# Which tiles the split planes of the last two FFN groups are put in

## The chip, the cores and the metric

The kernel runs on one core of a Trainium2 chip. The metric is device time in microseconds (us), as the median of the runs; lower is better. The engines are TensorE (PE in the profile; its weight loads are PEld), VectorE (DVE), ScalarE (ACT), GpSimd (POOL) and SyncE (SP, which issues DMAs).

## The reference

Eight batches of eight heads of attention over 576 tokens with 64 dimensions, in which scores below the row's maximum less `tau` are dropped, and then a feed-forward network (FFN) with an ELU over the 4608 tokens:

```python
scores = scale * np.matmul(q, k.transpose(0, 1, 3, 2))
thresh = np.max(scores, axis=-1, keepdims=True) - tau
scores = np.where(scores >= thresh, scores, -1000000000.0)
attn = softmax(scores)                       # written out in the reference
x = np.matmul(attn, v)                       # (8, 8, 576, 64) -> (4608, 512)
h = x @ w_in                                 # (512, 2048)
g = np.where(h > 0.0, h, np.exp(np.minimum(h, 0.0)) - 1.0)
return (g @ w_out).astype(np.float32)        # (2048, 512)
```

Everything is float32.

## The kernel before

**Groups.** The FFN is done in nine groups of 512 tokens. Groups 0 to 6 are worked beside the attention. Most of them use a Strassen scheme over sums of the weights' blocks. The change touches what comes last, groups 7 and 8 (`g7`, `g8` in the code), which run after the attention's last scores.

**Split planes.** Those two groups don't multiply in float32, which the rest of the FFN does. Each operand is split into planes of type float32r (`F32R`): `cut` (L2007, ACT) makes a scaled copy, `rest` (L2011, DVE) what that copy leaves out, `cross` (L2017, DVE) a mixture of both. For weights the same is done by `weights_cut` (L2028, ACT), `weights_rest` (L2032, DVE) and `weights_cross` (L2036, DVE). A product then is three matmuls of 128 x 128 by 128 x 512: cut by cut, rest by rest and cross by cross.

**The two rounds.** First every step (group, f) of the 16 blocks f of the hidden dimension: eight matmuls for cut and rest (`first_round`, L2203) and four for cross (`cross_round`, L2216) give h in one bank of PSUM; ACT scales the bank between them (L2207). ACT (exponential, L2227), POOL (L2230) and DVE (L2233) turn it into the raw activation, a float32 tile, which is split again. The two groups' steps are interleaved, so that planes of `w_in` made for group 7 serve group 8 a little later: 32 steps, 384 matmuls. Then the second round (`second`, L2278) multiplies the activations' planes with those of `w_out`, group 7 first, then group 8: 16 blocks times four token tiles times three matmuls for each group, 384 more. The first and last three blocks of a group (`EDGE = 3`) are taken together for each token tile. The stationary operand is a plane of `w_in` in the first round and of the activations in the second; the moving operand is a plane of x, and then of `w_out`.

**Order.** A planner writes the order out by hand. `at(t, f)` puts a piece of work on an agenda at a modelled time, `on_pe(cost, f)` does all that is due and then issues matmuls, `issued(key, x)` does more of the agenda until the plane that it is asked for is there. Nothing in it looks at which tile a plane got, so the order of instructions doesn't hang on tiles.

**Room.** A plane is 128 x 512, 2 KB a partition, and takes its room by `take`, which calls `slot(dt)`. There are two kinds of room:
- *Free slots*: 24 named `r0` to `r23`, opened where the attention's tiles were (L2069), and 34 named `l0` to `l33`, opened where the Strassen tiles were (L2139). They are kept in the queue `free`. A slot taken anew is a new tile over the old one's room.
- *Dead quarters*: once a weights' tile (`w_in0` to `w_in3`, `w_out0` to `w_out3`, four times 128 x 512 each) or a token tile `xt` isn't needed any more, `give` declares its room a new tile and puts its four quarters into `kept_for[dt]`. `kept_for[FP32]` serves raw activations, `kept_for[F32R]` the planes. The latter gets `w_out0` to `w_out3` as their blocks are split (`out_done`), and `w_in3` at the end of the first round's splitting (`in_done`). In the profile a float32r plane under the name `w_out` or `w_in` lies in such a quarter.

When its last matmul has been issued, `drop` puts a plane's room at the end of the queue that it came from, and the next taker gets the room at the front. The first instruction that writes a plane into such room waits until the matmul that read the earlier plane has ended.

Of the kernel before, what the change touches and what calls it, by code (L numbers as in the profile page):

```python
# [10 lines left out]
FP32 = mybir.dt.float32  # L11
# [357 lines left out]
def kernel(  # L369
# [1245 lines left out]
    with tc.manual_schedule():  # L1615
# [353 lines left out]

        EDGE = 3
        EPS, CUT = 2.0**-12, 1.0 - 2.0**-13
        free, kept_for, parts, split_stack = deque(), {FP32: deque(), F32R: deque()}, {}, ExitStack()

# [6 lines left out]
            kept_for[dt].extend(t[:, x] for x in range(KJ))  # L1982

        def slot(dt, wide=True):
            if kept_for[dt]:
                t = kept_for[dt].popleft()
                return t, lambda: kept_for[dt].append(t)
            pool, name = home = free.popleft()
            return pool.tile([P, DM], dt, name=name), lambda: free.append(home)

        def drop(key, *which):
            for x in which or range(len(parts[key])):
                parts[key][x][1]()
# [6 lines left out]
        def take(key, dt):  # L2000
            t = slot(dt)
            parts.setdefault(key, []).append(t)
            return t[0]
# [15 lines left out]
        def split_tokens(t, key, src, then=None):  # L2019
            at(t, lambda: cut(key, src))  # L2020
            at(t + 0.8, lambda: (rest(key, src), then and then()))
            at(t + 1.5, lambda: cross(key))
# [228 lines left out]
        def g_of(g, f):  # L2251
            def src():
                while (g, f) not in raw_g:
                    do_next()
                return raw_g[g, f]

            return src

        def start_f(t0, f):
            return t0 if f < EDGE else min(t0 + UNIT * f, t0 + UNIT * (NFT - EDGE))  # L2260

        OUT_EARLY = 11
        for f in range(NFT):
            split_weights(begin + 22.0 + 3.9 * f if f < OUT_EARLY else start_f(middle, f) - 9.0, ("out", f), w_out_of(f),
                          lambda f=f: out_done(f))
            for g, t0 in ((g7, middle), (g8, end)):
                t = start_f(t0, f) - (11.5 if f < EDGE else 6.0) + 3.2 * f * (f < EDGE)
                split_tokens(t, ("h", g, f), g_of(g, f), lambda g=g, f=f: drop(("g", g, f)))
# [41 lines left out]
        for g in (g7, g8):  # L2310
            for fs in (range(EDGE), *((f,) for f in range(EDGE, NFT - EDGE)), range(NFT - EDGE, NFT)):
                for i in range(4):
# [39 lines left out]
```

## Time and profile before

| | |
|---|---|
| median of 3 runs | 1260.25 us (1260.03 to 1261.15) |
| profiled execution | 1260.53 us, span 1258.8 us |
| TensorE busy | 1246.0 us (99%) |
| VectorE, ScalarE, GpSimd busy | 1041.6, 636.3, 729.1 us |
| granted TensorE clock | 1.00 |
| first matmul of group 7, last of group 8 | starts at 1076.7, starts at 1253.9 us |
| their 768 matmuls | 177.19 us of TensorE busy in 1077.0 to 1258.8 us |

Times in the profile count from the start of the span. The drained end of one matmul overlaps the start of the next, so a group of n matmuls in the timeline is shown longer than n starts: a single one is shown as 0.39 us, while starts are some 0.23 us apart. The chain of waits counts from end to end and doesn't have this overlap. "f<-r,l" names the tile written (f, a bank of PSUM), then the two tiles read without their numbers: moving operand, stationary operand.

### The profile page before, as it was taken

The page shows a single profiled execution, that of the slowest core. Times are in us where ns is not written, and L with a number is a line of the kernel's source. Part 1 is how long each engine was busy: PE and PEld are TensorE (multiplying, and loading weights), DVE is VectorE, ACT ScalarE, POOL GpSimd, SP SyncE. Part 2 cuts the span into 40 slices and gives each one's busy share as a digit, 9 for nine tenths or more (in the row PEclk, how much of TensorE's full clock was granted, in tenths as well). Part 3 has the DMA queues.
Part 4 walks back from the last instruction along what each step waited for, and adds up shares of the span by engine and source line. Part 5 has one row for each costly group of instructions (what it writes and reads, how often), then busy time and mean ns, then how long its engine had stood idle before and what let it go on. Part 6 is the DMA issues. An engine that isn't in the chain of part 4 may idle for free.

```text
span 1258.8 us, 21129 instructions
## 1 busy us (share of the span) xinstructions
PE 1246.0 (99%) x6598; PEld 956.6 (76%) x6598; DVE 1041.6 (83%) x2199; ACT 636.3 (51%) x1331; POOL 729.1 (58%) x1061
## 2 busy tenths in 40 slices
PE   8999999999999999999999999999999999999998
PEld 6676576477788787888788788778788887788876
DVE  6888778789898988898889889898889886876785
ACT  6989776664453526253534435352625352465321
POOL 4778655687575848676576757574867655122000
PEclk9999999999999999999999999999999999999999
DMA  7456688998989898998989888989899875000001
GB/s 138 147 175 178 175 244 219 274 255 226 235 236 260 241 249 232 235 257 220 269 206 259 226 241 219 261 242 251 231 234 257 221 232 173 20 1 1 1 34 34
DMA packets 325551, 245.74 MB, mean 195 GB/s; under 512 B 209216, under 2 KB 289984, under 8 KB 325440
## 3 DMA queue, kind: packets, MB, share of 16 engines
q1 hardware_dynamic: 323264, 243.65, 72.1%
q8 instruction: 52, 0.85, 0.3%
q10 hardware_dynamic: 2176, 0.75, 0.2%
q14 instruction: 59, 0.48, 0.1%
HBM read 154.53 MB, written 89.78 MB: 194 GB/s over the span
## 4 chain that ended last, share of the span: by engine, by line
PE 90%; DVE 3%; DMA 3%; ACT 1%; issue 1%; SPq 1%; POOL 1%; DVEq 0%; ACTq 0%; POOLq 0%
PE f L1678 22%; PE f L1818 22%; PE sc L977 8%; PE sc L1050 7%; PE f L2278 6%; PE f L2203 5%; PE f L1102 4%; PE sc L673 3%; PE f L1154 3%; PE f L2216 2%; PE pv L930 2%; PE rt L792 2%; PE sc L1042 1%; DMA there<-x 1%; PE sc L1037 1%
## 5 line engine op out<-in xcount | busy, mean ns | idle before, releaser
L984 DVE TENSOR_REDUCE mx<-sc 128x1 f32<-128x576 f32 x207 | 148.3, 750 | 28.3 <-PE sc L977 24.3
L726 POOL TENSOR_SCALAR w<-w,rs 128x576 f32<-128x576 f32 x144 | 116.3, 816 | 69.6 <-DVE rs L789 69.4
L1004 ACT ACTIVATE w<-sc,mx 128x576 f32<-128x576 f32 x113 | 81.5, 740 | 115.6 <-DVE mx L984 98.7
L868 DVE STREAM_TRANSPOSE x<-w 128x512 f32<-128x512 f32 (+1 forms) x153 | 108.9, 745 | 13.8 <-POOL w L726 11.8
L996 POOL TENSOR_SCALAR th<-mx,ntau 128x2 f32<-128x2 f32 (+1 forms) x114 | 34.0, 298 | 132.6 <-DVE mx L984 132.5
L977 PE MATMUL sc<-kT,qT 64*128 64x448 f32 (+4 forms) x736 | 103.1, 416 | 0.3 <-ACT xs L1066 0.3
L977 PEld LDWEIGHTS sc<-kT,qT 64*128 64x128 f32 x736 | 80.7, 186 | 25.2 <-issue 16.2
L1011 DVE SCALAR_TENSOR_TENSOR w<-sc,th,w 128x576 f32<-128x576 f32 x113 | 88.2, 810 | 9.4 <-ACT w L1004 9.2
L1678 PE MATMUL f<-xt,sw 128*128 128x256 f32 x384 | 93.4, 386 | 0.8 <-DVE g L1700 0.8
L1678 PE MATMUL f<-xt,w_in 128*128 128x256 f32 x384 | 92.3, 383 | 0.0
L1818 PE MATMUL f<-w_out,s 128*128 128x256 f32 x384 | 92.0, 382 | 0.1
L1818 PE MATMUL f<-w_out,g 128*128 128x256 f32 x384 | 92.0, 382 | 0.0
L1678 PE MATMUL f<-x,w_in 128*128 128x256 f32 x384 | 90.9, 379 | 0.0
L1818 PE MATMUL f<-t,s 128*128 128x256 f32 x384 | 90.8, 379 | 0.0
L726 POOL TENSOR_SCALAR e<-e,rs 128x576 f32<-128x576 f32 x91 | 67.4, 744 | 35.2 <-DVE rs L789 33.8
L1678 PEld LDWEIGHTS f<-xt,sw 128*128 128x128 f32 x384 | 69.4, 189 | 17.1 <-issue 4.5
L1678 PEld LDWEIGHTS f<-xt,w_in 128*128 128x128 f32 x384 | 71.7, 190 | 12.9 <-ACT w L1692 2.3
L1818 PEld LDWEIGHTS f<-w_out,g 128*128 128x128 f32 x384 | 72.0, 190 | 12.4 <-issue 3.1
L1818 PEld LDWEIGHTS f<-w_out,s 128*128 128x128 f32 x384 | 71.9, 190 | 12.5 <-issue 2.5
L1678 PEld LDWEIGHTS f<-x,w_in 128*128 128x128 f32 x384 | 72.8, 190 | 10.5 <-ACT s L1692 0.7
L1818 PEld LDWEIGHTS f<-t,s 128*128 128x128 f32 x384 | 72.8, 190 | 10.3 <-POOL s L1765 0.4
L1765 POOL TENSOR_TENSOR s<-g 128x256 f32<-128x256 f32 x96 | 75.0, 786 | 7.9 <-DVE g L1728 7.4
(349 smaller groups left out, 3113.7 us busy)
## 6 DMA issues: line engine op xcount, KB each, us to landing
there<-x SPq DMA_DIRECT2D x444, 144.0 KB, 3.5
wTb<-there SPq DMA_DIRECT2D x58, 576.0 KB, 6.5
wTa<-there SPq DMA_DIRECT2D x53, 576.0 KB, 5.0
sw<-win_sums SPq DMA_DIRECT2D x46, 384.0 KB, 4.9
t<-wout_sums SPq DMA_DIRECT2D x33, 512.0 KB, 6.1
qm<-in_q_dram SPq DMA_DIRECT2D x124, 72.0 KB, 4.8
wst<-in_moe_w_in_dram SPq DMA_DIRECT2D x16, 512.0 KB, 4.3
vm<-in_v_dram SPq DMA_DIRECT2D x64, 128.0 KB, 3.9
```

The costliest lines, as they stand in the source:

```text
L726: nc.gpsimd.tensor_scalar(wv, wv, st["rs"][:, h : h + 1], 1.0, ALU.mult, ALU.mult)
L868: nc.vector.transpose(x[:, :, c0 : c0 + nc_], src.rearrange("p (c g n) -> p g c n", c=nc_, n=T))
L977: on_banks(nc.tensor.matmul(o, qT[r, i * P : (i + 1) * P], kT[r, k0 : k0 + n], start=True, stop=True, skip_group_check=True), o)
L984: on_banks(nc.vector.tensor_reduce(st["mx"][:, h : h + 1], st["sc", h], axis=AX.XY if i == NC else AX.X, op=ALU.max, negate=True), st["sc" ...
L1004: on_banks(nc.scalar.activation(st["e", h], st["sc", h], AF.Exp, bias=st["mx"][:, h : h + 1]), st["sc", h])
L1011: on_banks(nc.vector.scalar_tensor_tensor(st["e", h], st["sc", h], st["th"][:, h : h + 1], st["e", h], ALU.is_ge, ALU.mult, accum_out=st[" ...
L1050: on_banks(nc.tensor.matmul(o, vm[:, h, c], parts[part][:, g0:g1, h * (NC + 1) + c], start=False, stop=(c == NC - 1), skip_group_check=Tru ...
L1678: nc.tensor.matmul(loc["banks"][place], left[:, j], right[:, j], start=(begins and j == 0), stop=(j == 1), skip_group_check=True)
L1765: engine.tensor_tensor(o, x, y, op)
L1818: nc.tensor.matmul(place(m), lhs, rhs, start=(begins and v == 0), stop=(v == RU - 1), skip_group_check=True)
L2203: nc.tensor.matmul(o, w.rearrange("p (j f) -> p j f", j=KJ)[:, j], m, start=(j == 0 and x == 0), stop=(j == KJ - 1 and x == 1), skip_group ...
L2278: nc.tensor.matmul(banks8[2 * i + x // 2], h[:, tok], w, start=(f == 0 and x != 1), stop=(f == NFT - 1 and x != 0), skip_group_check=True)
```

## The change

`slot` gave a plane a dead quarter whenever there was one, and a free slot otherwise. Now a float32r plane, which TensorE reads, takes a free slot, and a dead quarter only while no more than `RESERVE` = 2 free slots are left. Raw activations (float32) are served as before: a dead float32 quarter first, else a free slot.

```diff
-        EDGE = 3
+        EDGE, RESERVE = 3, 2
...
         def slot(dt, wide=True):
-            if kept_for[dt]:
+            if kept_for[dt] and (dt is FP32 or len(free) <= RESERVE):
                 t = kept_for[dt].popleft()
                 return t, lambda: kept_for[dt].append(t)
             pool, name = home = free.popleft()
             return pool.tile([P, DM], dt, name=name), lambda: free.append(home)
```

## The prediction

> **What bounds the kernel now.** The change acts only in the last two FFN groups, so I read the page for the engine totals, then the chain of waits for that stretch, then the timeline of TensorE by tile names, then the windows.
>
> The page, and then the chain that ended last (start, length, engine, line, count):
>
> ```profile
> span 1258.8 us, 21129 instructions
> PE 1246.0 (99%) x6598; PEld 956.6 (76%) x6598; DVE 1041.6 (83%) x2199; ACT 636.3 (51%) x1331; POOL 729.1 (58%) x1061
> ```
>
> ```profile
> 1115.99 1.81 PE f L2203 x8
> 1117.80 0.91 PE f L2216 x4
> 1118.71 1.87 PE f L2203 x8
> 1120.58 0.93 PE f L2216 x4
> ...
> 1164.77 27.42 PE f L2278 x118
> ...
> 1192.88 1.91 DVE l L2032 x3
> ...
> 1200.87 0.61 DVE r L2036
> ...
> 1201.53 52.76 PE f L2278 x226
> ```
>
> The reader should see two things. TensorE is the chain: matmuls follow one another from L2203 through L2216 to L2278, whose last piece ends at 1254.29; the 4.5 us from there to the end of the span are the last block's way out, which the change doesn't touch. And one matmul of the same shape doesn't always take the same time: eight L2203 matmuls take 1.81 us (226 ns each) at 1115.99 and 1.87 us at 1118.71, and 118 L2278 matmuls take 27.42 us (232 ns each). The page's "99% busy" hides this. So a change that makes no engine idle less may still shorten the span.
>
> Which tiles the longer ones read is in the timeline of TensorE. The second name after the arrow is the stationary operand, a single name means both come from tiles of that name; l and r are free slots, w_out and w_in in these lines are dead quarters of the weights' tiles:
>
> ```profile
> 1113.10 1.98 PE L2203 MATMUL f<-r,l 128*128 128x512 f32 x8
> ...
> 1118.55 2.03 PE L2203 MATMUL f<-r,w_out 128*128 128x512 f32 x8
> 1120.42 1.09 PE L2216 MATMUL f<-r,l 128*128 128x512 f32 x4
> ...
> 1124.06 1.98 PE L2203 MATMUL f<-r,r 128*128 128x512 f32 x8
> ```
>
> Every eight with slots alone take 1.98 us here (the last one's drain included), the eight with w_out 2.03, and the four that follow them 1.09 (0.93 against 0.91 in the chain), though they read a slot. That reads like a delay begun by the quarter and worked off after it. It is told apart from mere lateness by 1124.06, which is later and quick again. Why a quarter is slower to read no row shows.
>
> The windows give the stretch as blocks of equal content (length, TensorE busy, count of records touching the window, granted clock, DMA share, GB/s):
>
> ```profile
> 1091.35:1118.55 27.20, 27.20 (x122) 1.00 0.00 1
> 1118.55:1146.07 27.52, 27.52 (x121) 1.00 0.00 1
> 1146.07:1164.61 18.54, 18.54 (x82) 1.00 0.00 0
> 1164.61:1172.97 8.36, 8.36 (x38) 1.00 0.01 2
> 1172.97:1186.91 13.94, 13.94 (x62) 1.00 0.00 0
> 1186.91:1195.27 8.36, 8.36 (x38) 1.00 0.00 0
> 1195.27:1209.50 14.23, 14.15 (x61) 1.00 0.06 20
> 1209.50:1217.89 8.39, 8.39 (x38) 1.00 0.25 94
> 1217.89:1231.81 13.92, 13.92 (x61) 1.00 0.00 1
> 1231.81:1240.19 8.38, 8.38 (x38) 1.00 0.00 0
> 1240.19:1253.87 13.68, 13.68 (x60) 1.00 0.15 38
> ```
>
> The count has records draining over the edges; matmuls that start in the windows are 120, 120, 80, then 36, 60, 36, 60, 36, 60, 36, 59 (and the last at 1253.87). The first window has no operand in a quarter: 27.20 / 120 = 226.7 ns, my base. The granted clock is 1.00 throughout, so the excess is not throttling. Nor is it DMA: it is there at a DMA share of 0.00.
>
> The only idle time of TensorE behind the first group is this:
>
> ```profile
> 1201.05 0.40 PE L2278 MATMUL f<-l,w_out 128*128 128x512 f32 x1
> 1201.39 1.28 DVE L2036 TENSOR_TENSOR l<-l,w_out 128x512 fp32r<-128x512 f32 x2
> 1201.52 0.19 PEld L2278 LDWEIGHTS f<-r,r 128*128 128x128 f32 x1 [0.51 <-DVE r L2036]
> 1201.53 0.50 PE L2278 MATMUL f<-r,r 128*128 128x512 f32 x1
> 1201.86 0.39 PE L2278 MATMUL f<-w_out,w_in 128*128 128x512 f32 x1
> ```
>
> From 1201.05 to 1201.86 lie two starts that should take 0.46: the stall costs 0.35. The chain above says where it is from: ACT's weight planes (L2028) at 1192.22, then VectorE in one piece. ACT came late because its slot was just being read:
>
> ```profile
> 1192.22 1.68 ACT L2028 ACTIVATE w_out<-w_out 128x512 fp32r<-128x512 f32 x3 [2.15 <-PE f L2278]
> ```
>
> **The change part by part.** No instruction is added, removed or moved: in the changed program every engine has the same instructions in the same order, SP's and POOL's queues and all DMA issues too, only operands lie elsewhere. The two programs' operands, counted: of the 768 matmuls 396 read a quarter before (392 as stationary, 4 as moving operand alone), and 84 after (48 and 36). By the blocks above, before and after: 0 and 0; 36 and 0; 44 and 40; then 20 and 8; 52 and 0; 36 and 16; 44 and 0; 24 and 4; 56 and 0; 36 and 16; 48 and 0.
>
> *Pace.* The excess over 226.7 ns: block two 27.52 - 27.20 = 0.32 us; block three 18.54 - 80 x 0.2267 = 0.40; the eight L2278 blocks 89.26 - 383 x 0.2267 = 2.43. Together 3.15, of which 0.35 is the stall; 2.80 is pace, or 7.1 ns for each of the 392. What stays: the 48 stationary ones. Here they are scattered, so the delay behind each counts; I take 10 ns, from the eight at 1118.71 with what follows them (0.06 + 0.02 over eight; ends 7 and 11): 0.48 us. The 36 with the moving operand alone have hardly a row before (four matmuls). But a moving operand beside a stationary one adds nothing to see: the windows from 1172.97 and from 1240.19 have 48 stationary ones each and 20 against 32 moving ones, and both run at 232 ns. I take 3.5 ns, half of the 7, for 0.13 us, with ends 0 and 0.4 (11 ns each). The pace gains 2.80 - 0.48 - 0.13 = 2.19 us, all on the path, since TensorE is the chain.
>
> What carries this over to L2278 is the weak link: no long run of L2278 on slots alone exists before. The ends are nothing (L2278 is slower for its own reasons; then only L2203 and L2216 gain, 0.32) and the full 2.08 of its pace excess. I take the upper end less what stays, because L2278's matmul has the shape of L2203's, whose rows are the nearest.
>
> *Stall.* A quarter given back is taken again at once, so the next plane's writer waits for the reader; with some 58 slots in turn the last reader is long done. For the first of ACT's three at 1192.22 the changed program's last reader stands 47 matmuls further up in the order, about 11 us at 232 ns. The waits that go are a large part of these (total, times, longest):
>
> ```profile
> ACT w_out L2007 <- PE f L2278: 22.4, 8, 5.6
> ACT w_in L2007 <- PE f L2278: 16.0, 7, 5.3
> ```
>
> They are hidden behind TensorE, so they are worth nothing but the 0.35 at 1201.5. Late next would be VectorE's run of planes up to 1200.87; it begins with ACT's planes, which can come 2.15 earlier, more than the 1 us or so by which TensorE is then ahead (0.32 in block two, some 5 ns for each of about 150 matmuls of L2278). I count 0.35.
>
> *Reserve.* The float32 tiles of the raw activations take a dead float32 quarter first, as before, else one of the free slots, now with two left for them. I set each ACT and VectorE instruction's new last reader against this trace: no wait becomes tighter. Zero; the cover is ACT's idle half, and without it a stall costs about 0.35 like the one shown.
>
> Sum: 2.19 + 0.35 = 2.5 us. The profiled execution took 1260.53 (1.73 outside its span), which gives 1258.0; the median of the runs, 0.28 lower, gives 1257.7.
>
> **A rule that speaks against it.** The rows: 226 ns a matmul from slots, 234 with a stationary quarter. The Trainium skill, "TensorE: Matmul & The Clock Gate", Part 2 ("Step-by-step: what each phase is for" and "Back-to-back issue gap"), says that throughput is purely the N columns streamed, and gives N / 2.4 + 2.5, some 216 ns at N = 512, with no term for where an operand lies. By that rule only the stall would go, and an estimate of the time by it is the 1259.9 of the second rival; the trace disagrees on L2203, 1.81 against 1.87 for eight.
>
> **The rivals.**
> 1. L2278 has a floor of its own, about 230 ns (1195.27 to 1209.50 less the stall: 13.88 / 60 = 231 with mixed operands). Then its gain is 383 x 2 ns = 0.8, with 0.32 and 0.35 about 1.4: 1258.8. For: short stretches of slots inside L2278 aren't visibly quicker. Against: its neighbours there are all quarters, whose delay lasts.
> 2. The place of an operand is not what slows TensorE, but the neighbourhood in time; only the stall goes: 1259.9. For: the longer blocks are the late ones. Against: the quick eight at 1124.06, with longer ones before and behind.
> 3. Slower: slots run short. Planes now use up free slots sooner; a raw activation's exponential (L2227) must take a slot just dropped, waits for its matmul, and behind it in ACT's queue stand the scaling (L2207) and the planes' cuts, for which TensorE waits. At 0.35 a stall it outweighs the 2.5 gained and the 0.2% (2.5) from some 14 stalls on; one for each of the 16 steps of the last group costs 5.6 and nets 3.1: 1263.3. Against it: no new last reader stands later than the instruction that waits for it.
>
> **How the numbers follow.** The forecast's case has 0.77 (its own range 1257.1, where all 3.15 goes, to 1258.4), rival 1 0.09, rival 2 0.07, rival 3 0.07. A measurement of this kernel tells about 0.2%, 2.5 us, from no change: that is 1257.7, the middle of the first case, and I put a little over half of that case below it. So faster 0.44, within 0.2% 0.49 (the rest of the first case and rivals 1 and 2), slower 0.07. The range 1257.1 to 1259.9 leaves out the third rival, half of the second and a little below.
>
> **What would show it.** Right: in the chain all L2203 eights to about 1146 take 1.81, L2278's 384 matmuls about 87.5 us instead of 89.5, with l and r as names; the weight load waits for no VectorE at L2036; ACT's waits for L2278 fall below half. Pace wrong: L2278 on slots still at 230 or more. Stall wrong: another weight load waiting there. The prediction as a whole falls if TensorE shows new idle time between 1118 and 1254.

## The result, and the profile after

The changed kernel takes 1258.78 us (median of 21 runs, 1257.55 to 1260.45) against 1260.63 (21 runs, 1259.59 to 1262.03). The ratio is 0.9985 with a 95% interval of 0.9979 to 0.9991: 1.9 us less, between 1.1 and 2.6. That is a real gain, below the 0.2% that the prediction took as the bound.

The chain that ended last, in the changed kernel (start, length, engine, line, count):

```profile
1144.20 1.81 PE f L2203 x8
1146.01 0.91 PE f L2216 x4
1146.92 1.84 PE f L2203 x8
1148.76 0.94 PE f L2216 x4
...
1162.55 2.81 PE f L2216 x12
1165.36 87.70 PE f L2278 x384
1253.06 0.03 DVEq L2300
```

The eights of L2203 now take 1.81 us up to 1144.20, and longer ones come only in the block that still reads many quarters. L2278 is one unbroken piece: 384 matmuls in 87.70 us, where before there were 118 in 27.42, VectorE in between, and 226 in 52.76 up to 1254.29 (89.52 from the first to there). The profiled execution began its first matmul of the two groups at 1077.70, 1.04 later than that of before, in a part of the program in which nothing differs. Over the eleven profiles of this case that start lies between 1076.4 and 1079.5. So spans of single executions say little here. The stretch from the first to the last start of the 768 matmuls says more: it is 177.21 us before and 174.96 after, 2.25 less.

The windows with the same matmuls as those shown of before (length, TensorE busy, count, clock, DMA share, GB/s):

```profile
1092.36:1119.56 27.20, 27.20 (x122) 1.00 0.00 1
1119.56:1146.76 27.20, 27.20 (x122) 1.00 0.00 1
1146.76:1165.20 18.44, 18.44 (x81) 1.00 0.00 0
1165.20:1173.51 8.31, 8.31 (x37) 1.00 0.01 2
1173.51:1187.11 13.60, 13.60 (x61) 1.00 0.00 0
1187.11:1195.44 8.33, 8.33 (x37) 1.00 0.00 1
1195.44:1209.05 13.61, 13.61 (x61) 1.00 0.11 40
1209.05:1217.32 8.27, 8.27 (x37) 1.00 0.17 63
1217.32:1230.94 13.62, 13.62 (x61) 1.00 0.01 1
1230.94:1239.28 8.34, 8.34 (x38) 1.00 0.00 0
1239.28:1252.66 13.38, 13.38 (x61) 1.00 0.15 39
```

Every block without a quarter runs at the base pace: 27.20 for 120, 13.60 to 13.62 for 60. The four L2278 blocks of 36 with a few quarters are at 8.27 to 8.34, where 36 at the base pace take 8.16.

### The profile page after: what moved, and what is told of

It is laid out like the page before. It is cut to its first block, busy times and chain, and to the rows that moved or that the text cites. A ratio compares the mean times of both kernels' runs of the same rounds, so it can differ in the third digit from the quotient of the medians.

```text
span 1257.5 us, 21116 instructions
## 1 busy us (share of the span) xinstructions
PE 1243.9 (99%) x6598; PEld 957.0 (76%) x6598; DVE 1040.3 (83%) x2199; ACT 635.2 (51%) x1331; POOL 727.1 (58%) x1061
## 4 chain that ended last, share of the span: by engine, by line
PE 90%; DVE 3%; DMA 2%; ACT 2%; issue 1%; SPq 1%; POOL 1%; DVEq 0%; ACTq 0%; POOLq 0%
PE f L1678 23%; PE f L1818 22%; PE sc L977 8%; PE sc L1050 7%; PE f L2278 7%; PE f L2203 5%; PE f L1102 4%; PE sc L673 3%; PE f L1154 3%; PE f L2216 2%; PE pv L930 2%; PE rt L792 1%; PE sc L1042 1%; PE sc L1037 1%; DMA there<-x 1%
```

## The experiments

All are measured by the stretch of the 768 starts in one trace each, and four of them by the total time too. (The other five, e3, e4, e7, e8 and e9, ran once each for the trace: 1261.61, 1261.14, 1258.29, 1258.30 and 1261.65 us.) How far a stretch can be trusted shows in e7, e8 and the changed kernel, which turn out to be alike in pace and lie within 0.11 us of one another. Free slots start at 224 modulo 256 bytes, left and right ones alike; quarters start at 64. These places are counted from the order and the sizes of the program's tiles, as no row of the profile shows an address. The table says where each kernel puts them, and belongs to the sections below.

| kernel | l, r, quarters modulo 256 | matmuls that read a quarter | stretch, us |
|---|---|---|---|
| before | 224, 224, 64 | 396 | 177.21 |
| changed | 224, 224, 64 | 84 | 174.96 |
| e1 | 224, 224, 96 | 396 | 176.64 |
| e2 | 224, 224, 96 | 84 | 174.83 |
| e3 | 0, 192, 64 | 84 | 177.61 |
| e4 | 0, 224, 64 | 84 | 178.06 |
| e5 | 224, 224, 224 | 396 | 174.58 |
| e6 | 224, 224, 224 | 84 | 173.99 |
| e7 | 0, 0, 64 | 84 | 175.07 |
| e8 | 224, 224 (256 lower), 64 | 84 | 174.98 |
| e9 | 224, 96, 64 | 84 | 177.38 |

### e1 and e2: the quarters 32 bytes further

The prediction left open why a quarter takes longer to read. Quarters start at a multiple of 64 bytes, slots 32 bytes off one. One small constant moved ahead of the weights' tiles shifts the quarters and leaves the slots where they are; e1 does it to the kernel before, e2 to the changed one.

```diff
+    eight = const.tile([P, 1], I32, name="eight")
     w_in_sb = [const.tile([P, KJ, QF], FP32, name=f"w_in{x}") for x in range(4)]
...
-    eight = const.tile([P, 1], I32, name="eight")
```

> The kernel before, with one edit: a 32-byte constant is placed ahead of the weights' tiles instead of behind them, so that every dead quarter starts 32 bytes later and lies, like the free slots, 32 bytes off a multiple of 64. The choice between quarter and slot is that of before: 396 of the 768 matmuls still read a quarter. Theory A (the start address of the operand modulo 64 bytes sets the pace): all L2203 eights take 1.81 us, the matmuls of L2278 226.7 ns each, and the stretch from the first to the last of the 768 starts, 177.2 us before and 175.0 in the changed kernel, falls to 174.1 plus what a stall for late planes takes, since the waits for quarters given back remain (0.35 at least, up to 1.4 as TensorE arrives about 1 us earlier). Total about 2 to 2.8 us below before. Theory B (it is the kind of room or the region of memory, quarters of large tiles or low addresses): the eights with a quarter stay at 1.87 and the stretch at 177.2; no change of the total. Theory C (the waits of the planes' writers, not the reads, set the pace): as B.

> The changed kernel with the same 32-byte move of the weights' tiles. Theory A: the 84 matmuls that still read a quarter run at 226.7 ns too, so the stretch of the 768 starts falls from 175.0 to 174.1 us, 0.9 less than in the changed kernel, with no stall; total about 3 us below before. Theory B: the stretch stays at 175.0 and the total 1.9 below before. If the float32 matmuls of the other groups, which read the same weights' tiles, are also quicker with the move, the total falls by more than the stretch, the same in this run and in the one before it.

Measured: e1 takes 1259.76 us against 1260.93, ratio 0.9994 (0.9985 to 1.0003), its stretch 176.64; e2 takes 1258.25, ratio 0.9982 (0.9974 to 0.9991), its stretch 174.83. The chain of e1:

```profile
1118.76 1.81 PE f L2203 x8
1120.57 0.91 PE f L2216 x4
1121.49 1.86 PE f L2203 x8
1123.35 0.91 PE f L2216 x4
1124.25 1.81 PE f L2203 x8
```

The eight with a quarter at 1121.49 still take 1.86. Theory A, as it was put, has fallen: a place modulo 64 isn't what counts. But 0.57 us of the stretch did go, which "a quarter is a kind of room" (theory B) doesn't explain. The four behind the eight, 0.93 in the kernel before, take 0.91 here. e2 is near the 175.0 of theory B.

### e3 and e4: the slots moved

A pad of 32 bytes ahead of both blocks of slots (e3; left slots grow upwards, right ones downwards) or ahead of the left alone (e4), in the changed kernel:

```diff
         def open_slots(name, n, side):
+            if name in ("l", "r"):          # e4: ("l",)
+                split_stack.enter_context(tc.tile_pool(name=f"{name}pad", bufs=1, side=side)).tile([P, 8], FP32, name=f"{name}pad")
             pool = split_stack.enter_context(tc.tile_pool(name=name, bufs=1, side=side, reuse_waits="tile"))
```

> The changed kernel with a 32-byte pad ahead of each block of free slots, so that slots and quarters all start at a multiple of 64 bytes. 84 matmuls read a quarter as in the changed kernel, but all 768 now read both operands from multiples of 64. Theory A, absolute form (a start at a multiple of 64 is the slower one): all blocks at 230 to 234 ns, the stretch of the 768 starts at 176.5 to 179 us. Theory A, relative form (it is operands of unlike offset that cost, a difference of 32 between moving and stationary): all blocks at 226.7, the stretch at 174.1. Theory B: as in the changed kernel, 175.0 us, with the same blocks above 226.7.

> The changed kernel with the pad ahead of the 34 left slots (l) alone: l and the quarters start at multiples of 64 bytes, the 24 right slots (r) 32 off. Theory A, absolute form: matmuls with an l as stationary operand are now as slow as those with a quarter, the eights of L2203 with stationary l at 1.87 us and those with r alone at 1.81, the stretch at 176 to 178 us. Relative form: slow where l and r meet in one matmul. Theory B: 175.0 us.

The stretch is 177.61 in e3 and 178.06 in e4. The chain of e3, in a part where no quarter is read:

```profile
1095.09 1.85 PE f L2203 x8
1096.94 0.92 PE f L2216 x4
1097.86 1.87 PE f L2203 x8
1099.73 0.93 PE f L2216 x4
```

So slots alone can be as long to read as quarters (1.85 and 1.87 against 1.81), and theory B is out. The stretch of e3 is one that the absolute form expected, and that of e4 stands just above its 176 to 178. Taken alone, e3 would have looked like a proof of it, but e1 contradicts it, and so does a part of e4: its eight with r alone at 1119.33 take 1.86 us, where the absolute form had 1.81. What both kernels have in common with e1 is that operands of one matmul, or of neighbours, start at unlike places: the pads moved left and right slots apart. That is theory D.

### e5 and e6: the quarters where the slots are, modulo 512

Three small constants, 160 bytes, ahead of the weights' tiles; e5 is otherwise the kernel before, e6 the changed one:

```diff
+    eight, sm0, seen0 = const.tile([P, 1], I32, name="eight"), const.tile([P, 6, 2, 2], FP32, name="sm"), const.tile([P, 1], FP32, name="seen")
     w_in_sb = [const.tile([P, KJ, QF], FP32, name=f"w_in{x}") for x in range(4)]
...
-    eight = const.tile([P, 1], I32, name="eight")
...
-    totals, step_no = const.tile([P, 6, 2, 2], FP32, name="sm"), [0]
+    totals, step_no = sm0, [0]
...
-    seen = const.tile([P, 1], FP32, name="seen")
+    seen = seen0
```

> The kernel before, with its choice between quarter and slot (396 of 768 matmuls read a quarter), but three small constants (32 + 96 + 32 bytes) are placed ahead of the weights' tiles instead of behind, so that quarters start at 480 modulo 512 bytes, as the free slots do (before: 320; with the move by 32: 352). Theory D (formed after the first four runs: what costs is that operands read close together start at unlike places modulo 512 bytes): all blocks at 226.7 ns a matmul although quarters are read as often as before; the stretch of the 768 starts, 177.2 before, falls to 174.1 plus a stall, which remains because the writers' waits for quarters remain, 0.4 to 1.4: 174.5 to 175.5. Theory B (quarters as a kind of room, or low addresses): 176.6 to 177.2, eights with a quarter at 1.85 to 1.87.

> The changed kernel with quarters at 480 modulo 512 bytes, as the slots. Theory D: all 768 matmuls at 226.7, no stall, the stretch at 174.1 us against 175.0 in the changed kernel; total 0.9 below the changed kernel's and 2.7 to 3.2 below before. Theory B: 174.8 to 175.0, blocks with quarters at 229 to 232.

Measured: e5 1258.54 us against 1260.98, ratio 0.9979 (0.9970 to 0.9987), stretch 174.58. e6 1257.90, ratio 0.9977 (0.9967 to 0.9988), stretch 173.99. TensorE's timeline in e5, with the quarters of before:

```profile
1133.25 0.62 PE L2203 MATMUL f<-r,w_out 128*128 128x512 f32 x2
1133.71 1.52 PE L2203 MATMUL f<-l,w_out 128*128 128x512 f32 x6
1135.07 0.39 PE L2216 MATMUL f<-r,l 128*128 128x512 f32 x1
1135.29 0.84 PE L2216 MATMUL f<-l,l 128*128 128x512 f32 x3
1135.97 1.98 PE L2203 MATMUL f<-r,w_out 128*128 128x512 f32 x8
```

Eight with w_out take 1.98, and the six 1.52, as with slots: 396 matmuls read quarters and not one pays for it. The windows of e5 show what then is left:

```profile
1119.65:1146.85 27.20, 27.20 (x121) 1.00 0.00 1
1146.85:1164.99 18.14, 18.14 (x82) 1.00 0.00 0
1164.99:1173.15 8.16, 8.16 (x38) 1.00 0.01 2
...
1194.91:1209.07 14.16, 13.88 (x61) 1.00 0.06 20
```

and the wait of its weight load (timeline):

```profile
1200.50 0.69 DVE L2036 TENSOR_TENSOR r<-l,w_out 128x512 fp32r<-128x512 f32 x1
...
1201.10 1.29 DVE L2036 TENSOR_TENSOR l<-l,w_out 128x512 fp32r<-128x512 f32 x2
...
1201.24 0.19 PEld L2278 LDWEIGHTS f<-r,r 128*128 128x128 f32 x1 [0.70 <-DVE r L2036]
```

All blocks are at 226.7 ns but the one with the stall, 14.16 against 13.60: the stall is 0.56 there, where it was 0.35 before. Counted from the first of the 768 starts, TensorE gets to the matmul ahead of the stall 1.61 us earlier than before (122.78 against 124.39), and the weight load that waits for the plane begins only 1.41 earlier (123.45 against 124.86). In e6, with the change on top, that is gone and the whole stretch runs at the base pace:

```profile
1164.60 87.05 PE f L2278 x384
```

The move of the weights' tiles doesn't hasten the other groups: the two groups begin at 1077.8 and 1077.3 us, inside the spread named above.

### e7, e8 and e9: what has to be alike

The changed kernel with other pads ahead of the slots: 544 bytes left and 480 right (e7, all slots at a multiple of 512), 256 right alone (e8), 128 right alone (e9).

```diff
         def open_slots(name, n, side):
+            size = {"l": 544, "r": 480}[name] // 4     # e8: r alone, 256 bytes; e9: r alone, 128 bytes
+            split_stack.enter_context(tc.tile_pool(name=f"{name}pad", bufs=1, side=side)).tile([P, size], FP32, name=f"{name}pad")
             pool = split_stack.enter_context(tc.tile_pool(name=name, bufs=1, side=side, reuse_waits="tile"))
```

> The changed kernel with pads of 544 bytes ahead of the left and 480 bytes ahead of the right slots, so that all slots start at 0 modulo 512 instead of 480; quarters stay at 320 (84 matmuls read one). Theory D, relative: the blocks without a quarter at 226.7 as in the changed kernel, the stretch at 174.9 to 175.1. Theory D, absolute (480 modulo 512 is the one quick place): all blocks at 230 to 233, the stretch at 176.5 to 179.

> The changed kernel with a pad of 256 bytes ahead of the right slots alone: left slots at 480, right ones at 224 modulo 512, both at 224 modulo 256. If the places have to be alike modulo 256 only: as in the changed kernel, blocks without a quarter at 226.7, the stretch at 175.0. If modulo 512: the blocks of L2203 that mix l and r at 230 or more, the stretch at 176 to 178.

> The changed kernel with a pad of 128 bytes ahead of the right slots alone: left slots at 480, right ones at 352 modulo 512, alike modulo 128 and unlike modulo 256. If the places have to be alike modulo 256: blocks with l and r mixed at 229 to 232 from the first block on (226.7 in the changed kernel), eights of L2203 that read r and l at more than 1.81, the stretch of the 768 starts at 176 to 178 us. If alike modulo 128 is enough, and the 32-byte move of the quarters failed for another reason: 226.7 in the blocks without a quarter, the stretch at 175.0.

The chain of e7, of e8 and of e9, each at its first round:

```profile
1096.83 1.81 PE f L2203 x8
1098.64 0.91 PE f L2216 x4
1099.55 1.81 PE f L2203 x8
```

```profile
1096.94 1.81 PE f L2203 x8
1098.76 0.91 PE f L2216 x4
1099.66 1.81 PE f L2203 x8
```

```profile
1095.35 1.86 PE f L2203 x8
1097.22 0.93 PE f L2216 x4
1098.15 1.86 PE f L2203 x8
```

In e7 all slots lie where e3 had its left ones, at a multiple of 512, and the pace is the base's: no place is quick or long by itself, only likeness counts. A difference of 256 between left and right costs nothing (e8), one of 128 costs about as much as the others (e9, stretch 177.38). So, as far as these runs go, the start addresses have to be alike modulo 256 bytes; 32 apart (l and r in e4), 64 (e3), 128 (e9) and 160 (quarters and slots before) are all dearer.

## Why the prediction was right, and where its sizes were off

- *TensorE is the chain, and its pace hides behind "busy".* Right. The forecast of 1257.7 stands 1.1 us under the 1258.78 measured, inside the range; within 0.2%, the likeliest of its three cases, is what came. Of the 1.1, some 0.4 is the kernel before, whose median is 1260.63 in these runs and was 1260.25 in the three that the forecast started from; the other 0.7 is gain that didn't come. By the total alone rival 1, with 1258.8, fits better than the forecast. Only the blocks rule it out.
- *The pace carries over from L2203 to L2278* (the weak link, and rival 1). Right: blocks of L2278 without a quarter run at 13.60 / 60 = 226.7 ns. So there is no floor at 230, and that rival 1 names the measured total is chance. Rival 2, the neighbourhood in time, falls with e5, where the late blocks are as quick as the early ones.
- *The stall, 0.35 us.* Right: the weight load waits for no VectorE any more. e5 and e6 differ in the choice of room alone; e5, where only the pace was mended, keeps the stall, and e6 has none. So it comes with the old choice of room. That ScalarE's wait of 2.15 us is the link is read from the chain and was not tested by itself.
- *What stays.* This term was mis-sized. The prediction had 0.48 us for 48 stationary operands and 0.13 for 36 moving ones, 0.61 together. Measured against e6, block three keeps 18.44 - 18.14 = 0.30, the four mixed L2278 blocks 33.25 - 32.64 = 0.61, so 0.91 in all. The stationary ones come to 0.30 in block three and 8.31 - 8.16 = 0.15 in the first L2278 block, 0.45 against the 0.48. The moving ones alone are what was too cheap: 16 of them cost 8.33 - 8.16 = 0.17 us, 11 ns each (the upper end, where 3.5 were taken), and the four scattered in one block 0.11, 27 ns each, more than the upper end. The prediction compared blocks in which the stationary operand was unlike its neighbours anyway, and there a moving one more added nothing to see.
- *The sum.* In the stretch 2.54 was forecast and 2.25 measured; 0.30 of missing gain is that term. The total moved by 1.9 with an interval from 1.1 to 2.6, which holds 2.25; the rest of the gap is not told from the spread of the runs.
- *The writers' waits.* "Below half" was wrong. ScalarE's waits at L2007 and L2028 for L2278 went from 22.4 + 16.0 + 2.1 = 40.5 us to 26.2, 65% of what they were. With its reads of the finished banks (L2297, 17.1 us before and 36.1 after) they even rose, from 57.6 to 62.3:

```profile
ACT l L2007 <- PE f L2278: 11.4, 5, 3.7
ACT r L2007 <- PE f L2278: 10.7, 3, 4.6
...
ACT r L2028 <- PE f L2278: 4.1, 2, 2.3
```

  ScalarE, let go, runs ahead until the slots are used up and waits there instead. It costs nothing: TensorE stands behind none of them.
- *Rival 3, slots running short.* Not seen: the only weight load that waits in the changed kernel stands at 1077.69, at the very start of the two groups (0.39 us).
- *The rule that spoke against the change.* By a throughput of N columns alone the place could not matter; e5 and e9 settle that it does, 226.7 ns alike against 230 to 234 unlike. The Trainium skill, "TensorE: Matmul & The Clock Gate", Part 2, "Back-to-back issue gap", gives some 216 ns for 512 columns as the gap of a matmul by itself, and about 131 for a sustained stream of weight loads and matmuls. The measured pace decides: the best of these float32r matmuls, each with a weight load of its own, is 226.7 ns with everything alike. That is above both, and no run here shows why.
- *The reason that the prediction left open.* It spoke of quarters and slots. What the change does is narrower: it keeps operands at places that happen to be alike modulo 256. Moving the weights' tiles by 160 bytes gets more than the change does (stretch 174.58 against 174.96) with the old choice of room, and both together are the best here by the stretch, 173.99 us. The totals of 1258.54 (e5), 1257.90 (e6) and 1258.78 don't tell these three apart beyond the spread of the runs. That likeness counts and not the kind of room stands in the trace of the kernel before already. From 1242.74 on it reads quarters alone for a while; the first ten starts take 231 ns each, and then come four in 0.91 us, the base pace:

```profile
1245.05 0.39 PE L2278 MATMUL f<-w_out,w_out 128*128 128x512 f32 x1
1245.28 0.62 PE L2278 MATMUL f<-w_out 128*128 128x512 f32 x2
1245.73 0.39 PE L2278 MATMUL f<-w_out,w_out 128*128 128x512 f32 x1
1245.96 0.39 PE L2278 MATMUL f<-l,w_out 128*128 128x512 f32 x1
```

The runs changed the likeness of the moving to the stationary operand and that of successive reads together, but a part of e4 holds them apart. Fourteen matmuls in a row have their moving operand in r and their stationary one in l, so that neither changes its place:

```profile
1102.40 2.04 PE L2203 MATMUL f<-r,l 128*128 128x512 f32 x8
1104.28 1.09 PE L2216 MATMUL f<-r,l 128*128 128x512 f32 x4
1105.21 0.63 PE L2203 MATMUL f<-r,l 128*128 128x512 f32 x2
1105.68 1.55 PE L2203 MATMUL f<-l,l 128*128 128x512 f32 x6
```

Their starts are 234 ns apart to the last (3.28 us for fourteen). So a moving operand unlike the stationary one is enough. Nor does it take the other engines' reads and writes: in the kernel before, eight starts from 1245.96 to 1247.81, with slots and quarters mixed, are 231 ns apart, while VectorE and GpSimd do nothing and ScalarE works for 0.08 us.

What stays open: whether a change of place between matmuls that are alike in themselves costs too, and why the delay outlasts the unlike matmul by several. A delay that outlasts its cause needs no unlike operand: in e5, with everything alike, the four starts behind the stall (1201.57 to 1202.50) take 0.93 us, where four at the base pace take 0.91.

## What to carry to other kernels

Where TensorE is busy without a gap, count the starts of its matmuls block by block before looking for waits: 99% busy had 3 us in it here. When identical instructions take different times, note the addresses that they read, and move one thing by a few bytes; that is a smaller edit than a new policy and says more. A single experiment that agrees in size (e3) doesn't prove its theory, and it took e1, which moved the other kind of room, and e7, which moved all slots together, to tell place from likeness.

## What the runs showed of the hardware that was not expected

Matmuls of 128 x 128 by 128 x 512 in float32r start every 226.7 ns when the planes that are read all start alike modulo 256 bytes in their partitions, and every 230 to 234 ns when they don't. Offsets of 32, 64, 128 and 160 bytes were seen to cost this, 256 and the absolute place not. A moving operand unlike the stationary one is enough (fourteen in a row at 234 ns in e4). After eight unlike ones the next four, alike by themselves, still took 0.93 us instead of 0.91 in the kernel before, though not in e1.
